# Attention and a hard-swish feed-forward in one kernel: buffers handed out by the plan, other tile addresses, halved first loads and last stores

## Chip, cores and metric

The kernel runs on one core of a Trainium2 chip. The metric is the device time of one execution in microseconds, the median of several runs of the same built program. A profiled execution gives a trace of every engine and of the transfers.

## What is computed

Causal attention over 4 batches of 12 heads (448 positions, 64 wide), then a feed-forward layer on the 1,792 tokens: `h = x @ w_in`, `g = h * relu6(h + 3) / 6`, `out = g @ w_out`.

```python
def _attn_ref(q, k, v):                       # (4, 12, 448, 64) each
    scores = scale * np.matmul(q, k.transpose(0, 1, 3, 2))
    mask = np.triu(np.ones((seq, seq), dtype=bool), k=1)
    scores = np.where(mask, -1000000000.0, scores)
    scores = scores - np.max(scores, axis=-1, keepdims=True)
    attn = np.exp(scores)
    attn = attn / (np.sum(attn, axis=-1, keepdims=True) + 1e-09)
    return np.matmul(attn, v)

def _moe_ref(x, w_in, w_out):                 # (1792, 768), (768, 2048), (2048, 768)
    h = x @ w_in
    relu6 = np.clip(h + 3.0, 0.0, 6.0)
    g = h * relu6 / 6.0
    return g @ w_out
```

## The kernel before

**The work.** Attention goes in 24 units, each one batch and one pair of heads (`unit(b, p)`). A unit loads q, k and v, computes scores for four row tiles of 112 positions (tiles 3, 2, 1, 0 with 448, 336, 224, 112 columns; L464), takes row minima on VectorE (L479), exponentials with row sums on ScalarE (L486), inverses (L496, L497), scales the rows (L505, L507), transposes the probabilities on TensorE into PSUM banks (L527), copies them into d tiles (L346 on ScalarE, L349 on VectorE) and multiplies them with v (L540). The first six units multiply q and k in full float32 with operands in `gh`; the others split q and k into a rounded and a rest part, each in d tiles.

The feed-forward works on transposed activations. A product is a triple of matmuls of 448 columns in the rounded type: high weights by high input (L614), high by low (L615), low by high (L616). The weights lie in `wh` and `wl` (a few in `pr2`). The input halves lie in d tiles (`x`, `xc`, `gt`, `gm`), but in `gh` and `gl` for the products of `early_products`. Batch 0 goes through both layers while attention is still running, batch 1's second layer is mixed with later work in `middle`, batches 2 and 3 go through `last_first` and `last_second`, which combine block products with seven products in place of eight. The weights come as 64-bit words, are put together by VectorE in PSUM banks (`words`, L577, L579, L582) and kept in HBM (`kept_w`, sums in `kept_s`, activations in `kept_g`, `kept_x`) for later use.

**The order.** Nothing is issued as it is written. Each operation is handed to a planner, `Flow`, with a key (a due time), the engines that may run it and their costs. `Flow.run` lets a clock run, takes for each free engine the ready operation with the lowest key and writes out one order for all engines; tables of numbers at the head (`UNIT`, `LOADS`, `WORDS`, `T_*`, `K_*`) set the keys. All loads and stores go through SyncE's one queue, only three of the last stores through ScalarE's.

**Buffers.** A `Buf` is a tile with a tag; the tag names a pool: 22 buffers `d`, 8 PSUM banks `b`, 6 `wd`, 3 `wh`, and so on (`BUFS`, `BANKS`). The planner holds an operation back until enough buffers of its tags are free, and counts them only. When the order is written out, `ap` asks the pool for a tile of the tag, and the pool gives one of its buffers. The pools lie one after another in memory in the order const, gh, gl, prow, r, kl, vr, wh, wl, pr2, pr1, wd, d; `SHIFT` puts an unused pad ahead of some.

Of the kernel before, what the change touches and what calls it, by code (L numbers as in the profile page):

```python
# [30 lines left out]
T_FIRST = -87  # L31
T_PACE = 4.5
# [4 lines left out]
T_LOAD = -12  # L37
T_W = 10
T_WLOAD = 4
T_XA = 146  # L40
T_X = 172
T_LAST = 180
# [6 lines left out]
M_LOAD = 18  # L49
E_WORDS = 6.5  # L50
K_SCORES = 0
K_TURN = 7
K_TURNS = 0.4
K_PRODUCT = 10
K_GATE = 6
KEEP_FULL = 4
# [3 lines left out]
A_FIRST = 6  # L60
D_FIRST = 0
T_V = 11
# [3 lines left out]
UNIT = [-75, -37, -5, 7, 4, 3.5, -3.5, -3.5, 1.5, 0, -1.5, -1.5, -2, -5, -0.5, -5.5, -3, -1.5, -7, -7.5, 0.5, -2, 0, -2.5]  # L66
LOADS = [8, -8, 8, 6, 4, -10, 6, 12, -14, -14, -2, 0, -24, -10, 4, 2, 0, -18, 12, 6, -10, 10, -20, 12]
# [3 lines left out]
WORDS = [-1, 6, -1, 5, -8, 5, 7, -1, -1, -6, 8, -7, -6, -5, 6, 8, -7, -3, -5, 8, 7, -3, -7, -5, 2, 8, -2, -5]  # L71
T_ISSUE = 0.36
NORM_LAG = 2
# [6 lines left out]
SHIFT = dict(wh=112, d=112)  # L80
# [5 lines left out]
MOST = dict(qk=3, op=4, wf=6, sf=6, x=8, pt=9, pr3=5, pr20=3, xq=6, xc=21, gt=12, gm=8, so=3, s=8, most=7, ps=8, mo=4, c=8)  # L86
# [4 lines left out]
class Buf:  # L91
    def __init__(self, kind, shape, dt):
        self.kind, self.uses = kind, KINDS.get(kind, kind).split()
        self.tag = self.uses[0]
        self.shape, self.dt, self.tile, self.refs, self.held = shape, dt, None, 0, False
# [10 lines left out]
class Flow:  # L106
# [10 lines left out]
    DMA_PACKET, DMA_RATE, DMA_LANES, DMA_LATENCY = 0.010, 21e3, 16, 2.1  # L117

    def __init__(self, slots):
        self.free = dict(slots)  # L120
        self.filler, self.idle, self.spare = None, 0.0, 1
        self.ops, self.wrote, self.readers = [], {}, {}
# [29 lines left out]
    def run(self):  # L152
# [82 lines left out]
    def fill(self, now, out):  # L235

        n = int((now - self.idle - self.SPARE_TIME) / self.FILL)
        if self.spare and self.FILL_FROM < self.idle and now < self.FILL_UNTIL:
            b = Buf("b", [128, 512], F32)
            for i in range(n):  # L240
                out.append((self.idle + self.FILL * i, len(out), "PE", lambda _, m=self.mode: self.filler(b, m), set()))
# [45 lines left out]
def tile_causal_attention_hardswish_moe(ctx: ExitStack, tc: tile.TileContext, q, k, v, w_in, w_out, out):  # L287
# [116 lines left out]
    def unit(b, p):  # L404
# [11 lines left out]
        for a, src in enumerate((q, k)):  # L416
            dma(
                t + T_LOAD + LOADS[at], 4 * S, lambda a=a: qa(a),
                lambda src=src: src[b, p].rearrange("e d s -> (e d) s"), w=[kq[a]],
            )  # L420
# [46 lines left out]
        for a, two in enumerate(((3, 2), (1, 0))):  # L467
# [4 lines left out]
                reads + [("unit", at - (2 if b else DEPTH))], True,  # L472
# [195 lines left out]
    def store(key, m, g, v, o, queues=("SP",)):  # L668
        rows, n = out[128 * m:128 * m + 128].rearrange("m (g h w) -> m g h w", g=B, h=len(queues)), S // len(queues)
        for h, queue in enumerate(queues):  # L670
            dma(key, 4 * n, lambda h=h: rows[:, g, h], lambda h=h: v()[:, n * h:n * h + n], [o], (), queue)

    def sixth(key, o, ok, acc, s_, sk):
# [305 lines left out]
    def last_second(g):  # L979
# [128 lines left out]
```

## Time and profile before

| | |
|---|---|
| median of 3 runs | 591.88 us (591.71 to 592.56) |
| the profiled execution | 593.77 us, its span 592.0 us |
| mean granted clock of TensorE | 0.996 of full |
| busy share of the span: TensorE, VectorE, ScalarE, GpSimd | 98%, 83%, 68%, 39% |
| moved by transfers | 115.59 MB, mean 195 GB/s |

The span goes from the first to the last instruction of the program; the profiled execution has some time outside it. A matmul's row in the trace begins when it starts, and its end is modelled, so successive rows overlap: the pace of a stream is read from starts. In the views, PE is TensorE's matmuls, PEld its weight loads, DVE VectorE, ACT ScalarE, POOL GpSimd, SP SyncE (SPq its queue of transfers).

### The profile page before, as it was taken

Reading aid. Unit: us, or ns where it says so; the run is one execution under the profiler, and the core shown is the slowest. Engines: PE = TensorE matmul, PEld = TensorE weight load, DVE = VectorE, ACT = ScalarE, POOL = GpSimd, SP = SyncE. Lnnn points to the kernel's source line nnn. Section 1 sums busy time; section 2 is a strip of 40 time slices with the busy share of each in tenths; the row PEclk is TensorE's granted clock in tenths of the full one; section 3 lists DMA queues with packets and bytes.
Section 4 is the critical chain, followed back from the end, with each engine's and each line's share of the span. In section 5 each row is a group of like instructions: output and inputs, shape, how many; then the busy total and the mean of one; then the engine's idle time right before and its main releaser. Section 6 shows DMA issues by size and latency. Waiting matters only on the chain.

```text
span 592.0 us, 10667 instructions
## 1 busy us (share of the span) xinstructions
PE 579.1 (98%) x3484; PEld 501.1 (85%) x3484; DVE 492.6 (83%) x1099; ACT 403.2 (68%) x966; POOL 232.8 (39%) x223
## 2 busy tenths in 40 slices
PE   6999999999999999999999999999999999999997
PEld 3667988988888798878988888999999999999996
DVE  6999988799598899859998688998988799975641
ACT  6987888776668767679978796465555486454530
POOL 2757987764635554667453121043100042100000
PEclk9999999999999999989999999999999999999999
DMA  8936999996779899985834434422211424443411
GB/s 271 348 153 241 347 335 402 313 297 212 243 260 329 257 373 311 336 268 161 295 100 138 144 105 132 145 89 82 79 54 53 124 66 132 144 119 110 137 58 47
DMA packets 61064, 115.59 MB, mean 195 GB/s; under 512 B 6480, under 2 KB 36304, under 8 KB 61008
## 3 DMA queue, kind: packets, MB, share of 16 engines
q1 hardware_dynamic: 60576, 114.57, 58.0%
q8 instruction: 27, 0.44, 0.3%
q10 hardware_dynamic: 432, 0.34, 0.2%
q14 instruction: 29, 0.24, 0.1%
HBM read 83.39 MB, written 31.49 MB: 194 GB/s over the span
## 4 chain that ended last, share of the span: by engine, by line
PE 83%; DVE 7%; DMA 5%; ACT 4%; issue 1%; SPq 0%; DVEq 0%; ACTq 0%
PE b L614 22%; PE b L616 21%; PE b L615 21%; PE b L540 7%; PE b L527 6%; PE b L464 5%; DVE b L479 3%; DMA wd<-in_w_out_dram 3%; ACT d L486 1%; DMA gl<-kept_g 1%; DMA kept_w<-d 1%; DVE prow L479 1%; ACT gl L486 1%; DVE b L577 1%; DVE b L579 1%
## 5 line engine op out<-in xcount | busy, mean ns | idle before, releaser
L614 PE MATMUL b<-d,wh 128*128 128x448 f32 x624 | 233.3, 374 | 0.1
L616 PE MATMUL b<-d,wl 128*128 128x448 f32 x624 | 226.7, 363 | 0.0
L615 PE MATMUL b<-d,wh 128*128 128x448 f32 x624 | 225.9, 362 | 0.0
L346 ACT CAST wh<-wd 128x768 fp32r<-128x768 f32 x88 | 73.9, 839 | 77.9 <-PE b L615 74.2
L616 PEld LDWEIGHTS b<-d,wl 128*128 128x128 f32 x624 | 116.8, 187 | 10.8
L614 PEld LDWEIGHTS b<-d,wh 128*128 128x128 f32 x624 | 117.1, 188 | 10.4 <-DVE d L349 0.5
L615 PEld LDWEIGHTS b<-d,wh 128*128 128x128 f32 x624 | 117.2, 188 | 8.0
L358 DVE TENSOR_TENSOR wl<-wd,wh 128x768 fp32r<-128x768 f32 x73 | 76.5, 1049 | 25.3 <-ACT wh L346 24.0
L479 DVE CUSTOM_DVE_ANT_0 b<-b,mask 112x448 f32<-112x448 f32 (+1 forms) x192 | 80.1, 481 | 18.8 <-PE b L464 17.3
L486 ACT ACTIVATE d<-b,prow 112x448 f32<-112x448 f32 (+1 forms) x144 | 72.2, 515 | 12.9 <-DVE prow L479 12.8
L527 PE MATMUL b<-ident,d 112*112 112x112 f32 x384 | 54.5, 261 | 2.1 <-ACT d L486 1.4
L358 POOL TENSOR_TENSOR wl<-d,wh 128x768 fp32r<-128x768 f32 (+1 forms) x28 | 45.5, 1629 | 24.4 <-ACT wh L346 22.6
L527 PEld LDWEIGHTS b<-ident,d 112*112 112x112 f32 x384 | 41.9, 133 | 6.8 <-ACT d L486 1.9
L358 POOL TENSOR_TENSOR d<-d 128x896 fp32r<-128x896 f32 (+2 forms) x22 | 36.0, 1638 | 26.1 <-DVE wl L358 11.3
L346 ACT COPY d<-b 112x336 f32<-112x336 f32 (+1 forms) x92 | 38.8, 492 | 8.3 <-PE b L527 4.9
L507 POOL TENSOR_SCALAR d<-d,prow 112x112 f32<-112x112 f32 (+2 forms) x59 | 29.4, 509 | 30.7 <-ACT d L486 11.4
L464 PE MATMUL b<-d 64*112 64x448 f32 (+3 forms) x432 | 37.4, 311 | 1.6 <-ACT d L346 1.6
L505 ACT ACTIVATE d<-d,prow 112x112 f32<-112x112 f32 (+2 forms) x76 | 37.9, 551 | 1.4 <-DVE prow L497 1.2
L540 PE MATMUL b<-d,vr 112*64 112x224 f32 (+3 forms) x288 | 38.4, 410 | 0.0
L464 PEld LDWEIGHTS b<-d 64*112 64x112 f32 x432 | 30.7, 174 | 8.6 <-issue 2.4
L540 PEld LDWEIGHTS b<-d,vr 112*64 112x64 f32 x288 | 19.3, 138 | 19.9 <-issue 12.4
L358 DVE TENSOR_TENSOR d<-d 128x512 f32<-128x512 f32 (+3 forms) x44 | 32.7, 753 | 2.8 <-ACT d L346 1.5
(108 smaller groups left out, 942.6 us busy)
## 6 DMA issues: line engine op xcount, KB each, us to landing
wd<-in_w_in_dram SPq DMA_DIRECT2D x32, 384.0 KB, 6.2
wd<-in_w_out_dram SPq DMA_DIRECT2D x24, 512.0 KB, 6.4
wd<-kept_w SPq DMA_DIRECT2D x32, 384.0 KB, 3.9
wd<-kept_s SPq DMA_DIRECT2D x32, 384.0 KB, 3.1
kept_w<-d SPq DMA_DIRECT2D x16, 384.0 KB, 6.1
kept_w<-d SPq DMA_DIRECT2D x24, 256.0 KB, 4.8
kept_s<-d SPq DMA_DIRECT2D x24, 256.0 KB, 5.2
wd<-kept_w SPq DMA_DIRECT2D x48, 128.0 KB, 2.3
```

What stands on the lines that cost most here:

```text
L346: nc.scalar.copy(o(), i()) if scale is None else nc.scalar.mul(o(), i(), scale)
L358: (nc.gpsimd if e == "P" else nc.vector).tensor_tensor(o(), a(), b(), op)
L464: nc.tensor.matmul(score(e, i), qx[m, c], kx[m, :w], start=n == 0, stop=n == len(terms) - 1)
L479: lambda _, e=e, i=i, w=w: nc.vector.tensor_tensor_reduce(score(e, i), score(e, i), mask[:, S - w:], -0.125, 3.0e38, ALU.add, ALU.min, ap( ...
L486: lambda _, e=e, i=i: nc.scalar.activation(row_of(pr, e, i), score(e, i), ACTF.Exp, bias=ap(st)[:, e, i:i + 1], scale=-1.0, accum_out=ap(s ...
L505: nc.scalar.mul(x, x, ap(st)[:, e, 4 + i:5 + i])
L507: (nc.gpsimd if w == "P" else nc.vector).tensor_scalar(x, x, ap(st)[:, e, 4 + i:5 + i], 1.0, ALU.mult, ALU.mult)
L527: nc.tensor.transpose(ap(tp)[:C, C * n:C * n + C], row_of(pr, e, i)[:, C * j:C * j + C], ident)
L540: nc.tensor.matmul(ap(av)[64 * e:64 * e + 64, S - w:S], va()[:, j, e, :], ap(ph)[:, e, o:o + w], start=(j == 0), stop=(j == NC_ - 1),)
L614: nc.tensor.matmul(ps, ap(wh)[:, a], xh, start=start, stop=False, skip_group_check=more)
L615: nc.tensor.matmul(ps, ap(wh)[:, a], xl, start=False, stop=False, skip_group_check=more)
L616: nc.tensor.matmul(ps, ap(wl)[:, a], xh, start=False, stop=stop, skip_group_check=more)
```

## The change

Five things change together.

1. **Buffers.** Every buffer has a pool tag of its own (`d0`, `d1`, ...) with one buffer. The planner keeps a queue of free buffers for each tag, gives the one that came free first, and `ap` asks for that one.
2. **Transfers.** The planner's clock holds SyncE's queue until the eighth transfer before has landed (`QUEUE`), and its prices for a transfer are lower.
3. **Addresses.** `SHIFT` changes: a pad of 64 words (256 bytes) ahead of `gh`, 112 words ahead of `wh` as before, 16 words (64 bytes) in place of 112 (448 bytes) ahead of `d`.
4. **First loads and last stores.** The first unit's q and k are loaded in two halves each, columns 0 to 224 and 224 to 448, and its narrow row tiles (1, 0) come first. The last sums of `last_second` are computed and stored in halves of 224 columns, the first half through ScalarE's queue and the second through SyncE's.
5. **Tables.** Nearly all numbers that set keys, and the limits on how many buffers a kind may hold (`MOST`), are others.

```diff
-T_FIRST = -87
-T_PACE = 4.5
+T_FIRST = -120
+T_PACE = 4
...
-UNIT = [-75, -37, -5, 7, 4, 3.5, -3.5, -3.5, 1.5, 0, -1.5, -1.5, -2, -5, -0.5, -5.5, -3, -1.5, -7, -7.5, 0.5, -2, 0, -2.5]
+UNIT = [-88, -19, 3, 4, 2, 0, -1.5, -3, 4.5, 4, -2.5, -3, -3.5, -8, -2.5, -4.5, -2, -1.5, -6, -4.5, -2.5, 1, -4.5, 2]
...
-SHIFT = dict(wh=112, d=112)
+SHIFT = dict(gh=64, wh=112, d=16)
...
-MOST = dict(qk=3, op=4, wf=6, sf=6, x=8, pt=9, pr3=5, pr20=3, xq=6, xc=21, gt=12, gm=8, so=3, s=8, most=7, ps=8, mo=4, c=8)
+MOST = dict(qk=3, op=4, wf=4, sf=6, x=8, pt=7, pr3=5, pr20=4, xq=6, xc=21, gt=12, gm=9, so=3, s=8, most=8, ps=8, mo=4, c=8)
...
-    DMA_PACKET, DMA_RATE, DMA_LANES, DMA_LATENCY = 0.010, 21e3, 16, 2.1
+    QUEUE = 8
+    DMA_PACKET, DMA_RATE, DMA_LANES, DMA_LATENCY = 0.008, 23e3, 16, 2.1
 
     def __init__(self, slots):
         self.free = dict(slots)
+        self.slots = {t: deque(range(n)) for t, n in slots.items() if t in BUFS or t in BANKS}
...
                 elif what == "end":
                     left -= 1
-                    for b in x.bufs:
+                    for b in sorted(x.bufs, key=lambda b: b.at):
                         b.refs -= 1
                         if not b.refs:
+                            self.slots[b.tag].append(b.slot)
                             for t in b.uses:
                                 self.free[t] += 1
...
-        for b in o.bufs:
-            b.held = True
+        for b in sorted((b for b in o.bufs if not b.held), key=lambda b: b.at):
+            b.held, b.slot = True, self.slots[b.tag].popleft()
...
+        if e == "SP":
+            self.landed.append(o.ends[-1])
+            t = max([t, *self.landed[-self.QUEUE:-self.QUEUE + 1]])
         busy[e] = t
...
-            b.tile = pools[b.tag].tile(b.shape, b.dt, tag=b.tag, name=b.tag)
+            b.tile = pools[b.tag].tile(b.shape, b.dt, tag=f"{b.tag}{b.slot}", name=b.tag, bufs=1)
...
+        cuts = [(0, 2 * C), (2 * C, S)] if at == 0 else [(0, S)]
+        halves_ = [[(*x, h) for x in kq] for h in range(len(cuts))]
+        for h, (lo, hi) in enumerate(cuts):
+            for a, src in enumerate((q, k)):
+                dma(
+                    t + T_LOAD + LOADS[at], 4 * (hi - lo), lambda a=a, lo=lo, hi=hi: qa(a)[:, lo:hi],
+                    lambda src=src, lo=lo, hi=hi: src[b, p].rearrange("e d s -> (e d) s")[:, lo:hi], w=[halves_[h][a]],
+                )
...
-        for a, two in enumerate(((3, 2), (1, 0))):
+        for a, two in enumerate(((1, 0), (3, 2)) if at == 0 else ((3, 2), (1, 0))):
...
         def finish(key, m, h, o, ok, acc, s_, sk, queues=("SP",)):
-            sixth(key, o, ok, acc, s_, sk)
-            store(key + .5, m, 2 + h, o, ok, queues)
+            n = S // len(queues)
+            for a, queue in enumerate(queues):
+                c = slice(n * a, n * a + n)
+                sixth(key, lambda c=c: o()[:, c], (*ok, a), acc, lambda c=c: s_()[:, c], sk, c)
+                dma(
+                    key + .5, 4 * n, lambda c=c: out[128 * m:128 * m + 128, S * (2 + h):S * (3 + h)][:, c],
+                    lambda c=c: o()[:, c], [(*ok, a)], (), queue,
+                )
```

The order at the program's start, on SyncE's queue, where q, k and v of the first units are loaded into `gh` and `gl`. Before:

```order
L337 DMA gh<-in_q_dram 128x448
L337 DMA gh<-in_k_dram 128x448
L337 DMA gl<-in_v_dram 112x512
L337 DMA gh<-in_q_dram 128x448
L337 DMA gh<-in_k_dram 128x448
```

And now:

```order
L349 DMA gh<-in_q_dram 128x224
L349 DMA gh<-in_k_dram 128x224
L349 DMA gh<-in_q_dram 128x224
L349 DMA gh<-in_k_dram 128x224
L349 DMA gl<-in_v_dram 112x512
L349 DMA gh<-in_q_dram 128x448
```

The first two loads are two times two, and the first v and the second unit's q come two places later.

On TensorE around the first projection triples: scores (from `gh`), triples (from d and wh, wl), then transposes (with `ident`). Before:

```order
L464 MATMUL b<-gh 112x112 x2
L614 MATMUL b<-d,wh 128x448
L615 MATMUL b<-d,wh 128x448
L616 MATMUL b<-d,wl 128x448
L614 MATMUL b<-d,wh 128x448
L615 MATMUL b<-d,wh 128x448
L616 MATMUL b<-d,wl 128x448
L614 MATMUL b<-d,wh 128x448
L615 MATMUL b<-d,wh 128x448
L616 MATMUL b<-d,wl 128x448
L464 MATMUL b<-gh 112x448 x2
```

And now, in the new line numbers (L480 for scores, L543 for transposes, L630 to L632 for triples):

```order
L480 MATMUL b<-gh 112x336 x2
L630 MATMUL b<-d,wh 128x448
L631 MATMUL b<-d,wh 128x448
L632 MATMUL b<-d,wl 128x448
L543 MATMUL b<-ident,d 112x112
L543 MATMUL b<-ident,gl 112x112
L543 MATMUL b<-ident,d 112x112 x2
L543 MATMUL b<-ident,gl 112x112
L543 MATMUL b<-ident,d 112x112 x2
L630 MATMUL b<-d,wh 128x448
L631 MATMUL b<-d,wh 128x448
L632 MATMUL b<-d,wl 128x448
```

Three triples stood together; now they stand one by one between the transposes of a unit. So it goes on until attention ends: a change from a triple to a transpose stands 30 times in the order before and 53 times now. The numbers of triples (696), transposes (480), scores and products with v are the same.

At the program's end on VectorE, the sums of the last products with the parts that wait in d. Before, the last row of sums, and now:

```order
-L358 TENSOR_TENSOR wl<-wd,wh 128x768 x2
-L675 SCALAR_TENSOR_TENSOR d<-b,d 128x448 x3
+L370 TENSOR_TENSOR wl<-wd,wh 128x768 x2
+L689 SCALAR_TENSOR_TENSOR d<-b,d 128x224 x6
```

Three sums of 448 columns have become six of 224.

## Rows read from the trace of the kernel before

**Rows 1.** Busy time by stretches: us, busy and instructions by engine, clock, DMA.

```profile
core 0: us, PE busy (x) PEld busy (x) DVE busy (x) ACT busy (x) POOL busy (x), PEclk, DMA share, GB/s
0.00:40.00 40.00, 33.12 (x228) 21.62 (x228) 31.98 (x126) 32.04 (x109) 21.38 (x43) 1.00 0.85 285
40.00:180.00 140.00, 140.00 (x920) 120.24 (x921) 123.39 (x299) 105.54 (x266) 95.31 (x81) 1.00 0.82 287
180.00:260.00 80.00, 78.00 (x529) 64.58 (x528) 68.40 (x182) 58.78 (x162) 47.00 (x43) 0.98 0.93 316
...
366.00:588.00 222.00, 222.00 (x1100) 205.71 (x1098) 177.25 (x276) 115.15 (x194) 27.76 (x22) 1.00 0.32 100
...
240.00:260.00 20.00, 18.41 (x112) 14.86 (x111) 14.99 (x40) 12.60 (x34) 14.42 (x12) 0.91 0.95 328
```

**Rows 2.** TensorE in order of time, first and last start, 14 triples apart.

```profile
143.40 0.36 PE L614 MATMUL b<-gh,wh 128*128 128x448 f32 x1
...
151.80 0.36 PE L614 MATMUL b<-gh,wh 128*128 128x448 f32 x1
```

**Rows 3.** Line L614: count, ns least/median/most, first and last start.

```profile
L614 PE MATMUL b<-d,wh x624: 360/367/478, 33.4 to 587.5; 128*128 128x448 f32 x156
L614 PE MATMUL b<-gh,wh x48: 361/363/477, 128.2 to 168.6; 128*128 128x448 f32 x48
```

**Rows 4.** The chain that ended last, its start (at us, us, what); one issue.

```profile
1.23 2.69 DMA gh<-in_k_dram
...
4.05 1.86 PE b L464 x4
...
6.01 0.63 DVE b L479
...
10.15 0.68 ACT d L486 x4
...
2.16 0.43 SPq L337 DMA_DIRECT2D gh<-in_q_dram  x1
```

**Rows 5.** In order of time around 252 us, and the landing of the store.

```profile
252.22 0.78 ACT L346 COPY d<-b 112x336 f32<-112x336 f32 x2 [3.22 <-DMA gl<-kept_g]
...
252.71 2.17 PE L464 MATMUL b<-d 64*112 64x448 f32 x11 [1.59 <-ACT d L346]
...
245.86 0.37 SPq L337 DMA_DIRECT2D kept_s<-d  x1
...
DMA to landing us min/median/max: 6.2/6.2/6.2
```

**Rows 6.** TensorE in order of time around 194 us.

```profile
193.35 0.71 PE L527 MATMUL b<-ident,d 112*112 112x112 f32 x2
194.28 0.31 PE L527 MATMUL b<-ident,pr 112*112 112x112 f32 x1 [0.21 <-DVE d L582]
```

**Rows 7.** The last sum, and the last stores: count, KB, us to landing.

```profile
588.30 0.62 DVE L675 SCALAR_TENSOR_TENSOR d<-b,d 128x448 f32<-128x448 f32 x1 [1.81 <-PE b L616]
...
out_dram<-d SPq DMA_DIRECT2D x3, 112.0 KB, 1.8
out_dram<-d ACTq DMA_DIRECT2D x3, 112.0 KB, 2.0
```

**Rows 8.** VectorE's first narrow minimum in order of time.

```profile
8.08 0.43 DVE L479 CUSTOM_DVE_ANT_0 b<-b,mask 112x224 f32<-112x224 f32 x1
```

**Rows 9.** TensorE in order of time: ten transposes, two triples, transposes again.

```profile
88.09 0.26 PE L527 MATMUL b<-ident,d 112*112 112x112 f32 x1
...
88.57 0.64 PE L527 MATMUL b<-ident,d 112*112 112x112 f32 x5
...
90.29 0.26 PE L527 MATMUL b<-ident,d 112*112 112x112 f32 x1
```

**Rows 10.** TensorE's wait for loads; landing of the q load issued at 241.4.

```profile
PE b L464 <- DMA gh<-in_k_dram: 4.1, 1, 4.1
...
DMA to landing us min/median/max: 8.8/8.8/8.8
```

More of the change, by code (lines that the diff above doesn't have):

```diff
@@ L1 @@
 from bisect import insort
+from collections import deque
 from contextlib import ExitStack
@@ L36 @@
 T_DENSE = 7.25
-T_LOAD = -12
+T_LOAD = -18
 T_W = 10
-T_WLOAD = 4
-T_XA = 146
+T_WLOAD = 8
+T_XA = 163
 T_X = 172
-T_LAST = 180
+T_LAST = 182
 T_PAIR = 10.5
@@ L48 @@
 T_WORDS = 77
-M_LOAD = 18
+M_LOAD = 11
 E_WORDS = 6.5
 K_SCORES = 0
[L52 to L56, printed above, removed]
+K_TURN = 6.5
+K_TURNS = 0.6
+K_PRODUCT = 14
+K_GATE = 4
+KEEP_FULL = 0
 KEEP_TILED = 7
@@ L59 @@
 DEPTH = 3
-A_FIRST = 6
+A_FIRST = 4.8
 D_FIRST = 0
-T_V = 11
+T_V = 15
 FINE = 3
@@ L65 @@
 W_BEHIND = 4
-UNIT = [-75, -37, -5, 7, 4, 3.5, -3.5, -3.5, 1.5, 0, -1.5, -1.5, -2, -5, -0.5, -5.5, -3, -1.5, -7, -7.5, 0.5, -2, 0, -2.5]
-LOADS = [8, -8, 8, 6, 4, -10, 6, 12, -14, -14, -2, 0, -24, -10, 4, 2, 0, -18, 12, 6, -10, 10, -20, 12]
+UNIT = [-88, -19, 3, 4, 2, 0, -1.5, -3, 4.5, 4, -2.5, -3, -3.5, -8, -2.5, -4.5, -2, -1.5, -6, -4.5, -2.5, 1, -4.5, 2]
+LOADS = [-6, -64, -24, 12, -14, -2, 6, -12, -6, -10, -4, -16, -10, 12, 2, 6, -12, 8, -2, -8, 2, 2, 0, 12]
 K_KEEP = -4
@@ L70 @@
 GATE_FROM = 1
-WORDS = [-1, 6, -1, 5, -8, 5, 7, -1, -1, -6, 8, -7, -6, -5, 6, 8, -7, -3, -5, 8, 7, -3, -7, -5, 2, 8, -2, -5]
+WORDS = [2, 3, 0, 8, -8, 5, -6, 4, 3, 3, 1, 3, 8, 5, -2, -8, 8, 6, 2, -7, -7, 3, 7, 7, 4, 0, -1, 1]
 T_ISSUE = 0.36
-NORM_LAG = 2
+NORM_LAG = 1.5
 A_LAG = 0
@@ L85 @@
 )
-MOST = dict(qk=3, op=4, wf=6, sf=6, x=8, pt=9, pr3=5, pr20=3, xq=6, xc=21, gt=12, gm=8, so=3, s=8, most=7, ps=8, mo=4, c=8)
+MOST = dict(qk=3, op=4, wf=4, sf=6, x=8, pt=7, pr3=5, pr20=4, xq=6, xc=21, gt=12, gm=9, so=3, s=8, most=8, ps=8, mo=4, c=8)
 ORDERED = dict(sf=3, wd=0, wh=1, wl=2, xq=3, xc=3, gt=3, gm=3, pr3=4, pr2=5, pr1=6, pr20=9, pt=7, op=8)
 class Buf:
+    made = 0
     def __init__(self, kind, shape, dt):
@@ L94, in __init__ @@
         self.tag = self.uses[0]
-        self.shape, self.dt, self.tile, self.refs, self.held = shape, dt, None, 0, False
+        self.shape, self.dt, self.tile, self.slot, self.refs, self.held = shape, dt, None, None, 0, False
+        Buf.made += 1
+        self.at = Buf.made
 class Op:
@@ L116 @@
     KEEP = KEEP_FULL, KEEP_TILED
-    DMA_PACKET, DMA_RATE, DMA_LANES, DMA_LATENCY = 0.010, 21e3, 16, 2.1
+    QUEUE = 8
+    DMA_PACKET, DMA_RATE, DMA_LANES, DMA_LATENCY = 0.008, 23e3, 16, 2.1
     def __init__(self, slots):
         self.free = dict(slots)
+        self.slots = {t: deque(range(n)) for t, n in slots.items() if t in BUFS or t in BANKS}
         self.filler, self.idle, self.spare = None, 0.0, 1
-        self.ops, self.wrote, self.readers = [], {}, {}
+        self.ops, self.wrote, self.readers, self.landed = [], {}, {}, []
     def op(self, key, ways, parts, r=(), tiled=False, nbytes=0):
@@ L237, in fill @@
         n = int((now - self.idle - self.SPARE_TIME) / self.FILL)
-        if self.spare and self.FILL_FROM < self.idle and now < self.FILL_UNTIL:
+        if self.spare and self.slots["b"] and self.FILL_FROM < self.idle and now < self.FILL_UNTIL:
             b = Buf("b", [128, 512], F32)
+            b.slot = self.slots["b"][0]
             for i in range(n):
@@ L301, in tile_causal_attention_hardswish_moe @@
             ctx.enter_context(tc.tile_pool(name=f"shift_{tag}", bufs=1)).tile([128, SHIFT[tag]], F32, name=f"shift_{tag}")
-        pools[tag] = ctx.enter_context(tc.tile_pool(name=tag, bufs=bufs))
+        pools[tag] = ctx.enter_context(tc.tile_pool(name=tag, bufs=1))
     for tag, bufs in BANKS.items():
-        pools[tag] = ctx.enter_context(tc.tile_pool(name=tag, bufs=bufs, space=bass.MemoryType.PSUM))
+        pools[tag] = ctx.enter_context(tc.tile_pool(name=tag, bufs=1, space=bass.MemoryType.PSUM))
     flow = Flow({**BUFS, **BANKS, **MOST})
@@ L415, in unit @@
             qa, kq = lambda a: ap(first_qk)[:, 2 * p + a], [(first_qk, 2 * p + a) for a in range(2)]
[L416 to L420, printed above, removed]
+        cuts = [(0, 2 * C), (2 * C, S)] if at == 0 else [(0, S)]
[6 more added lines that the diff above has]
+                )
+        kq = [x for y in halves_ for x in y]
         dma(t + T_LOAD + LOADS[at] + T_V, 512 * NC_, va, lambda: v[b, p], w=[kv], rows=C)
@@ L471, in unit @@
                 [(cost * C * (i + 1) + more, lambda i=i: products(i), [(ps[e, i][0], i) for e in range(2)] + [("turn",)]) for i in two],
-                reads + [("unit", at - (2 if b else DEPTH))], True,
+                (halves_[0] if at == a == 0 else reads) + [("unit", at - (2 if b else DEPTH))], True,
             )
@@ L666, in first_layer, with store, sixth @@
         return out if g else (gh, gl)
[L668 to L673, printed above, removed]
+    def store(key, m, g, v, o):
+        dma(key, 4 * S, lambda: out[128 * m:128 * m + 128, S * g:S * g + S], v, [o])
+    def sixth(key, o, ok, acc, s_, sk, c=slice(0, S)):
         def emit(_):
-            nc.vector.scalar_tensor_tensor(o(), ap(acc)[:, :S], 1.0 / 6.0, s_(), ALU.mult, ALU.add)
-        one(key, {"D": 1}, elem(S), emit, [(acc, 0), sk], [ok])
+            nc.vector.scalar_tensor_tensor(o(), ap(acc)[:, c], 1.0 / 6.0, s_(), ALU.mult, ALU.add)
+        one(key, {"D": 1}, elem(c.stop - c.start), emit, [(acc, 0), sk], [ok])
     def snap_m(key, o, ok, acc):
```

## The prediction

> **What bounds the kernel now.** I read the busy time by stretches first [rows 1]. TensorE works in all of 366 to 588 us (222.00 of 222.00) and in all of 40 to 180 (140.00 of 140.00); it misses 6.9 us before 40 and 2.0 between 180 and 260, and the last sum starts only at 588.30 [rows 7]. No other engine is full over a whole stretch: VectorE has 177 of the last 222 us. So after 40 us TensorE's own pace sets the end, and a change can gain in three places: the pace of a matmul, the start, the waits in the middle.
>
> The pace is read from starts, since the durations in the rows overlap. The projections go in triples of matmuls of 448 columns (L614 to L616), and after 366 there is nothing else: 1098 weight loads are 366 triples in 222.00 us, 0.6066 each [rows 1]. From 143.40 to 151.80 there are 14 triples: 8.40 / 14 = 0.6000 us [rows 2]. Shapes, types and granted clock (1.00) are the same; the first read their moving operand from tile d, the second from gh and gl. 624 triples read d (a few more have their weights in pr), 48 read gh and gl [rows 3].
>
> The start is a chain: k's load is issued at 1.23 us and takes 2.69, the four first records of the scores 1.86, then VectorE's row minima from 6.01, and ScalarE's exponentials of the unit until 10.83 [rows 4].
>
> In the middle the largest wait stands at 252.71: TensorE idles 1.59 us for a bank, ScalarE having idled 3.22 us before it could copy transposes into a d tile at 252.22 [rows 5]. The row names a load of kept_g; but a store kept_s<-d, issued at 245.86, took 6.2 us [rows 5] and so landed at about 252.06, when the copy could start. I read it so: the copy had been given the d buffer that this store was still reading. Behind the wait the clock fell to its lower level (1.2 GHz): the mean grant of the 20 us around is 0.91 [rows 1], so 0.09 x 20 = 1.8 us of full-speed time were withheld, part of it while TensorE idled. A second wait is a transpose at 194.28 that waits for VectorE's words to leave a bank: it starts 0.93 us after the pair before it began at 193.35 [rows 6], while two transposes want 0.19 (five in 0.48 from 88.09, [rows 9]).
>
> **The change, part by part.** *Same work.* The two orders hold the same matmuls, loads and stores but for the cuts named below, and move some copies between VectorE, ScalarE and GpSimd.
>
> *Other addresses.* The padding ahead of d shrinks from 448 to 64 bytes. As built, d begins at byte 147,648 of a partition before and 147,520 now, wh at 96,000 and 96,256, gh at 19,264 and 19,520. The distance from wh to d was 51,648 = 201 x 256 + 192 and is 51,264 = 200 x 256 + 64; from wh to gh it is -300 x 256 + 64 in both, to gl -188 x 256 + 64. Tiles and half tiles (3,584 and 1,792 bytes) are whole multiples of 256, so every d operand had remainder 192 and now has 64, which gh and gl had all along. If the pace hangs on the remainder, 624 triples gain 6.6 ns each: **-4.1 us**. Bounds: 0 (the pace belongs to the other layout of gh and gl) and -4.3 (the few with weights in pr too). I take -4.1, since gh and d triples stand in one stage with one kind of weights, and the remainder is what I find to differ besides the name.
>
> The Trainium skill ("TensorE: Matmul & The Clock Gate", Part 2, step 1) says that TensorE has two independent read ports, so that loading the next weights takes nothing from the running matmul; "SBUF — State Buffer", Who interferes with whom, says that TensorE waits on nobody. By that, the place of d against wh would not matter and this term would be 0. The trace has two paces in one execution [rows 1, 2], which these pages do not explain.
>
> *Halved first loads.* The first k load is still the second issue (1.23 us), but 112 KB instead of 224. Nearest rows: a 112 KB store lands in 1.8 us, this 224 KB load in 2.7 [rows 4, 7]; I take 2.25, so scores begin 0.45 earlier (0 to 0.9). The first product has 224 columns where it had 448, half of 1.86 us: 0.9 earlier again. So VectorE starts at about 4.7, not 6.01. It then does its four short minima (0.43 and less each, [rows 8]) until about 6.0 and waits for the wide product: the second half of k is the fourth issue (2.16, [rows 4]) and lands at 4.4, before the short products end at about 5.0; 5.0 + 1.86 = 6.9. The four wide minima (6.01 to 8.08 now, [rows 4, 8], 2.1 us) end near 9.0; before, the short ones then followed until 9.2. But ScalarE, which was 1.6 us behind VectorE at 10.83 with the short exponentials, has done these and has one or two wide ones left, some 1.0 us by estimate, so the unit's exponentials end at about 10.0: **-0.8 us**, bounds 0 and -1.8 (all of VectorE's earlier start). This goes to the end one for one if nothing in the first 40 us absorbs it, since TensorE is full after.
>
> *The order of the first 40 us.* Triples now stand between single banks of transposes, where they fill gaps. Idle there besides the first 4.05 is 2.8 us [rows 1]; I take **-0.5**, bounds 0 and -2.8. The price of the splitting: ten transposes and two triples take 2.20 us (88.09 to 90.29), while 10 x 0.096 (five in 0.48) and 2 x 0.607 are 2.17 [rows 9]; 0.03 us for a block, 23 blocks more in the whole order (53 changes from a triple to a transpose, 30 before): **+0.7**, bounds 0.3 and 0.9.
>
> *Buffers chosen by the plan.* Until now the plan only counted free buffers, and which one a tile got was the pool's affair. Now the plan hands out the one that has been free longest by its own clock, and that clock holds a transfer back until the eighth before it has landed. The wait at 252 is of the kind that this removes: 1.59 idle and half of the 1.8 of withheld clock, **-2.5 us**. Bounds: 0, and -5 if the wait at 194 (0.7), the rest of the 2.0 idle and the rest of the clock go too. What is late next is then VectorE, 0.86 busy in that stage [rows 1].
>
> *Halved last stores.* The last sum of 448 columns took 0.62 us, then two stores of 112 KB land in 1.8 (SP) and 2.0 (ACT) [rows 7]. Now ACT's store leaves after half the sum, some 0.23 earlier (the difference of 448 and 224 columns: 0.63 - 0.43 is 0.20, [rows 4, 8]), and SP's leaves some 0.15 later but is the shorter: **-0.1**, bounds -0.2 and +0.2.
>
> Sum: -4.1 - 0.8 - 0.5 + 0.7 - 2.5 - 0.1 = -7.3 us. The profiled execution took 593.77 (span 592.0, the rest outside), 1.9 above the median 591.88 of the runs; differences carry over, so 591.9 - 7.3 = **584.6 us**.
>
> **Rivals.** *The remainder means nothing.* The fast triples differ also in that their two halves lie in two tiles. Then -4.1 falls away: 588.7. For it: the rows differ in both respects. Against it: a second tile is only another address, which is what the remainder is too. 0.15. The pages named above stand on this rival's side.
>
> *Time given back before 366.* TensorE comes earlier to a stage in which transfers (0.93 of their time between 180 and 260) and VectorE set the pace; the early gains become waits. What stays is behind 366, where TensorE is full with 366 triples: 366 x 6.6 ns = 2.4 and the tail 0.1: 589.4. For it: ScalarE and VectorE waits in [rows 5, 6]; against it: TensorE is full from 40 to 180 and the waits between 180 and 260 are 2.0 in all [rows 1]. 0.13.
>
> *A late load: slower.* In the new order all q and k loads stand at other places of SP's one queue. With the queue full, a q load takes 8.8 us to land [rows 10]; SP's later transfers wait behind it, ScalarE or GpSimd waits to split it, and the scores behind them. If one pair comes a full queue late in the stage 180 to 260 with no triples left to fill, the price is up to 8.8; with the other terms (-4.8 without the wait at 252) 595.9. It decides from a wait of 4.8 us on. Against it: TensorE waited for a load only once, 4.1 us at the start [rows 10]. 0.09.
>
> *The pools do nothing.* The d buffer was free anyway, other waits arise as large: -2.5 and -0.5 fall away, 587.6. 0.05.
>
> **How the numbers follow.** The forecast has 0.58 and stands for 580 to 588. A run of this kernel tells 0.2% (1.2 us) from no change. Faster: the forecast 0.58, the pools' rival 0.05, nine tenths of the remainder's (0.13), two thirds of the time given back (0.09): 0.85. Same 0.07, from the rest of these two and the light end of the late load; slower 0.08. Range: 579.5 (head and middle at their better bounds in part) to 590.0, which takes in the rivals at 588.7 and 589.4 and leaves out the late load and the tails, under 0.2.
>
> **What would show it.** Starts of 33 triples behind 366: 19.80 us apart (right) or 20.02. First score near 3.6 and first minimum near 4.7 us; the first unit's exponentials done near 10.0. Between 180 and 366 no idle above 0.5 us on TensorE and a granted clock of 1.00. A wrong prediction would show as new idle time on TensorE before scores (L480) with a load as releaser, or as triples at 0.607.

## The result and the profile after

The changed kernel took 586.63 us (median of 4 runs, 585.31 to 588.1), the kernel before 592.22 beside it (591.71 to 592.56): a ratio of 0.9907, 95% interval 0.9881 to 0.9933, or 5.6 us less. 584.6 had been forecast, with 579.5 to 590.0 as the range. The profiled execution took 586.24, its span 584.1; that of before 593.77 and 592.0. So the two profiled executions differ by 7.5 us, near the 7.3 of the forecast's sum, and the medians by 5.6: the profiled execution of before lay 1.55 above its median, that of the changed kernel 0.4 below.

Busy time by stretches of the changed kernel, to be laid beside [rows 1]:

```profile
core 0: us, PE busy (x) PEld busy (x) DVE busy (x) ACT busy (x) POOL busy (x), PEclk, DMA share, GB/s
0.00:40.00 40.00, 31.49 (x213) 20.40 (x214) 31.41 (x125) 29.57 (x102) 22.38 (x43) 1.00 0.91 274
40.00:180.00 140.00, 139.65 (x936) 119.61 (x936) 120.69 (x309) 108.63 (x282) 101.29 (x89) 1.00 0.78 272
180.00:260.00 80.00, 79.82 (x548) 67.79 (x546) 69.90 (x170) 60.95 (x165) 47.52 (x42) 1.00 0.96 324
240.00:260.00 20.00, 20.00 (x139) 16.43 (x140) 19.69 (x43) 17.67 (x46) 14.84 (x13) 1.00 1.03 355
```

Three things are to be seen. The stage from 180 to 260 has lost its idle time (79.82 busy, 78.00 before) and its fall of the clock (1.00 in 240 to 260, 0.91 before). The first 40 us have become worse, not better: TensorE works 31.49 us of them, and it worked 33.12. And what the busy time can't tell, the pace, stands in the starts. TensorE in order of time, two triples 33 apart:

```profile
399.99 0.36 PE L630 MATMUL b<-d,wh 128*128 128x448 f32 x1
...
419.79 0.36 PE L630 MATMUL b<-d,wh 128*128 128x448 f32 x1
```

33 triples in 19.80 us are 0.6000 each, the pace that only gh and gl had before [rows 2].

The start, from the timelines of TensorE, VectorE and ScalarE (start, duration, what, idle time ahead and its releaser):

```profile
3.48 3.69 PE L480 MATMUL b<-gh 64*112 64x224 f32 x16 [3.48 <-DMA gh<-in_k_dram]
8.69 2.15 PE L480 MATMUL b<-gh 64*112 64x448 f32 x16 [1.53 <-DMA gh<-in_k_dram]
...
23.77 1.57 PE L480 MATMUL b<-gh 64*112 64x448 f32 x6 [1.33 <-DVE d L598]
...
5.06 0.40 DVE L495 CUSTOM_DVE_ANT_0 b<-b,mask 112x224 f32<-112x224 f32 x1 [3.41 <-PE b L480]
...
9.57 0.56 ACT L502 ACTIVATE d<-b,prow 112x336 f32<-112x336 f32 x1
```

The first score starts at 3.48 (4.05 before), the first minimum at 5.06 (6.01) and the unit's last exponential ends at 10.13 (10.83, [rows 4]). So far the halves did nearly what was forecast. But then TensorE waits 1.53 us for the second unit's k, which it had not waited for, and 1.33 us at 23.77 for VectorE to leave a bank. VectorE was late there itself: it had waited for a load before each half of the first weight's words, and the words keep the bank. The same words before, and now:

```profile
19.17 1.05 DVE L577 TENSOR_SCALAR b<-wd 128x384 int32<-128x384 int32 x2
```

```profile
20.72 0.56 DVE L593 TENSOR_SCALAR b<-wd 128x384 int32<-128x384 int32 x1 [1.19 <-DMA wd<-in_w_in_dram]
21.77 0.56 DVE L593 TENSOR_SCALAR b<-wd 128x384 int32<-128x384 int32 x1 [0.49 <-DMA wd<-in_w_in_dram]
...
23.17 1.01 DVE L598 SCALAR_TENSOR_TENSOR d<-wd,b 128x384 int32<-128x384 int32 x2
```

The chain that ended last shows the same of the next weight. Behind the first scores it was VectorE's and ScalarE's work before [rows 4], and now its start is transfers, each issued when another one ahead of it had landed:

```profile
5.96 6.57 DMA gh<-in_q_dram
...
12.55 7.13 DMA gl<-in_v_dram
...
19.69 9.29 DMA wd<-in_w_in_dram
...
29.00 0.56 DVE b L593
```

VectorE begins the second half of the second weight's words only at 29.00, when this load has landed.

### The profile page after: what moved, and what is told of

It reads as the page before. It is cut to its first block, busy times and chain, and to the rows that moved or that the text cites. A ratio compares the mean times of both kernels' runs of the same rounds, so it can differ in the third digit from the quotient of the medians.

```text
span 584.1 us, 10651 instructions
## 1 busy us (share of the span) xinstructions
PE 571.7 (98%) x3484; PEld 500.3 (86%) x3484; DVE 485.5 (83%) x1091; ACT 402.9 (69%) x970; POOL 240.0 (41%) x230
## 3 DMA queue, kind: packets, MB, share of 16 engines
HBM read 83.39 MB, written 31.49 MB: 197 GB/s over the span
## 4 chain that ended last, share of the span: by engine, by line
PE 91%; DMA 4%; DVE 2%; ACT 2%; SPq 1%; issue 0%; DVEq 0%
PE b L630 24%; PE b L631 24%; PE b L632 24%; PE b L556 7%; PE b L543 6%; PE b L480 6%; DMA wd<-in_w_in_dram 2%; DMA gl<-in_v_dram 1%; DMA gh<-in_q_dram 1%; ACT d L502 1%; SPq L349 1%; DVE b L595 0%; DVE b L593 0%; ACT gl L502 0%; DVE d L598 0%
## 5 line engine op out<-in xcount | busy, mean ns | idle before, releaser
L630 PE MATMUL b<-d,wh 128*128 128x448 f32 x624 | 231.4, 371 | 0.2 <-ACT d L502 0.2
L632 PE MATMUL b<-d,wl 128*128 128x448 f32 x624 | 225.5, 361 | 0.0
L630 PEld LDWEIGHTS b<-d,wh 128*128 128x128 f32 x624 | 117.2, 188 | 10.5 <-issue 0.7
L632 PEld LDWEIGHTS b<-d,wl 128*128 128x128 f32 x624 | 116.8, 187 | 8.3
L370 DVE TENSOR_TENSOR wl<-wd,wh 128x768 fp32r<-128x768 f32 x70 | 72.7, 1039 | 28.7 <-ACT wh L358 27.8
L495 DVE CUSTOM_DVE_ANT_0 b<-b,mask 112x224 f32<-112x224 f32 (+1 forms) x192 | 80.2, 480 | 12.4 <-PE b L480 10.7
L502 ACT ACTIVATE d<-b,prow 112x448 f32<-112x448 f32 (+2 forms) x144 | 72.3, 516 | 15.6 <-DVE prow L495 13.8
L543 PE MATMUL b<-ident,d 112*112 112x112 f32 x384 | 56.1, 260 | 1.1 <-ACT d L502 0.8
L358 ACT COPY d<-b 112x336 f32<-112x336 f32 (+1 forms) x103 | 44.4, 487 | 12.8 <-PE b L543 8.3
L370 POOL TENSOR_TENSOR d<-d 128x896 fp32r<-128x896 f32 (+3 forms) x24 | 39.7, 1658 | 22.3 <-PE b L543 10.5
L370 POOL TENSOR_TENSOR wl<-wd,wh 128x768 fp32r<-128x768 f32 x18 | 33.1, 1841 | 35.3 <-ACT wh L358 33.5
L543 PEld LDWEIGHTS b<-ident,d 112*112 112x112 f32 x384 | 42.8, 133 | 5.0 <-POOL gl L523 1.0
L523 POOL TENSOR_SCALAR d<-d,prow 112x336 f32<-112x336 f32 (+2 forms) x62 | 33.0, 543 | 15.3 <-DVE prow L513 13.1
L370 POOL TENSOR_TENSOR d<-gh,d 128x448 fp32r<-128x448 f32 x8 | 9.6, 1201 | 71.3 <-DVE gh L370 55.6
L593 DVE TENSOR_SCALAR b<-wd 128x384 int32<-128x384 int32 (+1 forms) x56 | 33.2, 615 | 4.9 <-DMA wd<-in_w_in_dram 3.0
L521 ACT ACTIVATE d<-d,prow 112x112 f32<-112x112 f32 (+2 forms) x69 | 34.0, 528 | 4.5 <-DVE prow L513 4.2
L480 PEld LDWEIGHTS b<-d 64*112 64x112 f32 x432 | 30.2, 172 | 6.0 <-issue 2.0
```

The source lines that it names most:

```text
L358: nc.scalar.copy(o(), i()) if scale is None else nc.scalar.mul(o(), i(), scale)
L370: (nc.gpsimd if e == "P" else nc.vector).tensor_tensor(o(), a(), b(), op)
L480: nc.tensor.matmul(score(e, i), qx[m, c], kx[m, :w], start=n == 0, stop=n == len(terms) - 1)
L495: lambda _, e=e, i=i, w=w: nc.vector.tensor_tensor_reduce(score(e, i), score(e, i), mask[:, S - w:], -0.125, 3.0e38, ALU.add, ALU.min, ap( ...
L502: lambda _, e=e, i=i: nc.scalar.activation(row_of(pr, e, i), score(e, i), ACTF.Exp, bias=ap(st)[:, e, i:i + 1], scale=-1.0, accum_out=ap(s ...
L521: nc.scalar.mul(x, x, ap(st)[:, e, 4 + i:5 + i])
```

## The experiments

Each run has the kernel before beside it on the same chip; ratios are to that. Differences in us are of medians; the ratios and their intervals are worked out from all the runs, and since the kernel before has more runs in which the clock fell than some of the others, they can show about 1 us more. The address and pool kernels were chosen so that the order of instructions stays what it is, engine by engine, and only the cause in dispute differs.

**The place of d.** Four kernels. One number in the kernel before:

```diff
-SHIFT = dict(wh=112, d=112)
+SHIFT = dict(wh=112, d=16)
```

> The kernel before with one number changed: the pad ahead of d is 16 words, not 112, so that d begins 64 bytes (and not 192) past a multiple of 256 counted from wh; the order of every engine is that of before. Theory A (the remainder sets the pace): 33 triples behind 366 us are 19.80 us apart, not 20.02, and the time is 592.2 - 4.1 = 588.1. Theory B (gh and gl were faster for another reason, the place of d means nothing): 20.02 and 592.2.

Measured: 589.32 us, ratio 0.9942 (0.9918 to 0.9967), 2.9 less; three of the six runs, with a mean granted clock of 0.999 or more, took 588.1 to 588.5. And the number put back in the changed kernel:

```diff
-SHIFT = dict(gh=64, wh=112, d=16)
+SHIFT = dict(gh=64, wh=112, d=48)
```

> The changed kernel with d's pad at 48 words, so that d has its old remainder of 192 from wh; the order and the pools are those of the changed kernel. Theory A: triples of d at 0.6066 us again and 586.6 + 4.1 = 590.7. Theory B: 0.600 and 586.6. If the new pace comes from the pools or from the order, B's numbers too.

Measured: 589.34, ratio 0.9953 (0.9925 to 0.9981), 2.7 more than the changed kernel had taken on its own chip. Starts of 33 triples, of the first kernel and of the second:

```profile
399.95 0.36 PE L614 MATMUL b<-d,wh 128*128 128x448 f32 x1
...
419.75 0.36 PE L614 MATMUL b<-d,wh 128*128 128x448 f32 x1
```

```profile
399.79 0.36 PE L630 MATMUL b<-d,wh 128*128 128x448 f32 x1
...
419.81 0.36 PE L630 MATMUL b<-d,wh 128*128 128x448 f32 x1
```

19.80 and 20.02 us: the pace follows the pad, in either order and with either kind of pools. The rival that the remainder means nothing is out. Whose remainder it is, the third kernel asks, with `wh=144` in the place of `wh=112`:

> The changed kernel with wh's pad at 144 words, not 112: wh, wl and d all move by 128 bytes, gh and gl stay. d's own address now has remainder 192 (that of before), but its distance from wh still 64; gh's own remainder stays 64, but its distance from wh becomes 192. Theory A1 (the distance between the moving operand and the weights counts): d triples stay at 0.600, the 48 of gh and gl go to 0.607, 586.6 + 0.3 = 586.9. Theory A2 (the moving operand's own address counts): d triples go to 0.607, gh's stay at 0.600, 590.7.

Measured: 585.6, ratio 0.9884 (0.9866 to 0.9902). Two triples 33 apart that read d, and two 12 apart that read gh and gl:

```profile
399.64 0.36 PE L630 MATMUL b<-d,wh 128*128 128x448 f32 x1
...
419.44 0.36 PE L630 MATMUL b<-d,wh 128*128 128x448 f32 x1
...
154.68 0.36 PE L630 MATMUL b<-gh,wh 128*128 128x448 f32 x1
...
161.96 0.36 PE L630 MATMUL b<-gh,wh 128*128 128x448 f32 x1
```

d stays at 19.80 / 33 = 0.6000, and gh, which nobody moved, goes to 7.28 / 12 = 0.6067. The distance between the moving operand and the weights counts, not the operand's own place. This kernel also gives the term its best timing, since the kernel with `d=48` ran on the same chip: 589.34 - 585.6 = 3.7 us, and 576 more slow triples (624 of d less 48 of gh and gl) at 6.6 ns are 3.8. The fourth kernel has `d=0`, a distance of whole multiples of 256:

> The changed kernel with no pad ahead of d: its own remainder is 0 and its distance from wh is 0 too. No row of before has this case. Theory A: if what counts is that moving operand and weights don't fall on the same place, the triples are at 0.607 or more and the time is 590.7 or more. Rival: any remainder but 192 is as good, 0.600 and 586.6.

Measured: 590.68, ratio 0.9976 (0.9947 to 1.0005).

```profile
399.55 0.36 PE L630 MATMUL b<-d,wh 128*128 128x448 f32 x1
...
419.61 0.36 PE L630 MATMUL b<-d,wh 128*128 128x448 f32 x1
```

20.06 / 33 = 0.6079, the slowest of the three remainders that were tried (64, 192, 0), and the time is that of theory A. The remainder 128 was not tried.

**The pools.** Part 1 alone in the kernel before (its core; the free queues are those of the change's diff):

```diff
-            b.tile = pools[b.tag].tile(b.shape, b.dt, tag=b.tag, name=b.tag)
+            b.tile = pools[b.tag].tile(b.shape, b.dt, tag=f"{b.tag}{b.slot}", name=b.tag, bufs=1)
```

> The kernel before with part 1 alone: every buffer a pool of its own, given out by the plan; the planner's prices, the tables and the order of every engine are those of before, instruction for instruction, and so are the addresses. Theory P (the middle waits come from the pool giving a buffer that is still being read): the wait of 1.59 us at 252 and the one at 194 go, no idle time over 0.5 us between 180 and 366; where the clock doesn't fall before either, 592.2 - 2.5 = 589.7. Rival (the plan's own clock is wrong and the waits belong to the order): the wait at 252 stands, 592.2.

Measured: 590.29, ratio 0.994 (0.9915 to 0.9966), 2.7 less. Busy time of the stretch in which the 1.59 us were lost, and ScalarE's copies there, which came 3.22 us late before [rows 5]:

```profile
240.00:260.00 20.00, 20.00 (x129) 17.22 (x130) 16.28 (x46) 14.70 (x44) 15.40 (x14) 1.00 1.01 362
...
250.52 0.78 ACT L354 COPY d<-b 112x336 f32<-112x336 f32 x2 [0.41 <-PE b L535]
```

TensorE is busy in all of it, at the full clock, and the copies wait for TensorE's transposes alone. So a buffer was what they had waited for. All buffers changed at once, but two transfers alone come into question, the load that the row in [rows 5] names and the store that the forecast took in its place. The load's issue and landing before, and the store's with the pools:

```profile
246.91 0.32 SPq L337 DMA_DIRECT2D gl<-kept_g  x1
...
DMA to landing us min/median/max: 5.7/5.7/5.7
```

```profile
245.66 0.37 SPq L345 DMA_DIRECT2D kept_s<-d  x1
...
DMA to landing us min/median/max: 6.6/6.6/6.6
```

The load landed at 252.6, after the copies had begun at 252.22, so they had not waited for it. The store still lands late with the pools, at 252.3, but the copies begin at 250.52 without it. That fits the buffer under the store; which buffer a tile got, no trace names. Both parts together, the pools and `d=16`, in the old order with the old loads and stores:

> The kernel before with part 1 and the new place of d (pad 16 words), the old order, loads and stores. If the two terms add: 592.2 - 3.5 (d's new place as measured alone, 592.2 to 588.4 where the clock was full) - 2.5 = 586.2, the whole gain without the new tables and the halved loads. If the changed kernel's gain needs its tables: 588.5.

Measured: 586.71, ratio 0.988 (0.9837 to 0.9924). The two terms add (0.9942 x 0.994 = 0.988), and they are as much as the whole change. Then the other way round, the changed kernel with the old pools (the line above taken back):

> The changed kernel with the old pools (22 buffers of d in one pool, 8 banks in one, and so on, given in turn); the order of every engine is that of the changed kernel, instruction for instruction. Theory P: buffers come late, waits on TensorE of 2.5 us or more in all return between 40 and 366, 586.6 + 2.5 = 589.1. Rival (the new tables and the queue of eight made the order good, the pools give nothing): 586.6.

Measured: 585.57, ratio 0.9857 (0.9811 to 0.9902), not slower than the changed kernel. TensorE's waits of this kernel between 180 and 366 us (total, times, longest):

```profile
PE b L630 <- ACT d L502: 0.7, 1, 0.7
PE b L543 <- DVE d L598: 0.2, 1, 0.2
PE b L480 <- DVE gh L665: 0.2, 1, 0.2
```

1.1 us in all and no fall of the clock. The changed kernel itself waits 0.2 there in its first profile, but in a second one (of its repetition, below) it is 1.35 short of the 186 us, with waits of 0.70 and 0.57:

```profile
180.00:366.00 186.00, 184.65 (x1255) 159.19 (x1254) 159.49 (x385) 149.69 (x394) 94.06 (x82) 1.00 0.74 245
...
188.99 0.28 PE L543 MATMUL b<-ident,d 112*112 112x112 f32 x1 [0.57 <-DVE d L598]
```

So the old pools wait no more than the new ones in this order. Theory P holds in the old order and falls in the new one: there the transfers and copies meet no buffer that is still being read for long, whoever gives it.

**The first loads.** The changed kernel, the first unit's q and k sent whole, VectorE's, ScalarE's and TensorE's order untouched:

```diff
-                    t + T_LOAD + LOADS[at], 4 * (hi - lo), lambda a=a, lo=lo, hi=hi: qa(a)[:, lo:hi],
-                    lambda src=src, lo=lo, hi=hi: src[b, p].rearrange("e d s -> (e d) s")[:, lo:hi], w=[halves_[h][a]],
+                    t + T_LOAD + LOADS[at], 4 * (hi - lo), lambda a=a: qa(a),
+                    lambda src=src: src[b, p].rearrange("e d s -> (e d) s"), w=[halves_[h][a]], skip=h == 1,
```

With `skip` the second half's transfer is left out.

> The changed kernel, but the first unit's q and k come as two transfers of 224 KB, not four of 112; the order of all engines but SyncE is unchanged, SyncE's later transfers go out two places earlier. Theory L (the two more places cost more than the earlier first score gives): the first score starts at 4.05 and not 3.48, the second unit's k lands 0.9 us earlier than 8.56, and TensorE gets to the first projection about 1 us earlier; 585.6 or the same as the changed kernel within the measurement. Rival (the halves bring what they were forecast to bring): 586.6 + 0.8 = 587.4.

Measured: 583.86 (583.8 to 585.25), ratio 0.9837 (0.9793 to 0.9881), the lowest of all. (It ran on the chip of the pools' kernels, without the changed kernel beside it; the intervals of the two ratios touch at 0.9881.) Its first 40 us, its waits for loads there, and the chain's weight load:

```profile
0.00:40.00 40.00, 34.78 (x237) 23.05 (x238) 33.51 (x134) 31.17 (x108) 24.99 (x47) 1.00 0.86 274
...
PE b L480 <- DMA gh<-in_k_dram: 4.1, 1, 4.1
...
13.12 7.00 DMA wd<-in_w_in_dram
20.21 0.57 DVE b L593
```

The first score starts 0.6 later (4.09), and TensorE then never waits for k again; the second half of the first weight's words, the chain's here, begins at 20.21 (21.77 with the halves), TensorE does not wait for them, and it works 34.78 us of the 40, 3.3 more than with the halves. How much of this is the halves and how much one execution's luck, the other kernels tell: with halved columns TensorE worked between 30.58 and 34.38 us of the first 40 in seven profiled executions (mean 32.6), with the old order 33.1 to 33.3 in four, with whole loads in the new order 34.78 and 34.70. In two of the seven the clock fell within the 40 us, and there the same work is busy for longer. Both profiles with whole loads are of the shortest execution of their kernel. Faster loads alone don't explain them, though: the kernel with `wh=144`, with halves, moved 272 GB/s in its first 20 us, the one with whole loads 265, and still worked 1.0 us less of the 40:

```profile
0.00:20.00 20.00, 14.61 (x98) 10.15 (x99) 14.27 (x62) 14.94 (x54) 8.37 (x22) 1.00 0.92 272
0.00:40.00 40.00, 33.76 (x236) 22.88 (x237) 33.36 (x132) 31.17 (x108) 24.84 (x47) 1.00 0.86 274
```

```profile
0.00:20.00 20.00, 14.98 (x91) 9.47 (x92) 14.27 (x62) 14.22 (x53) 8.38 (x22) 1.00 0.92 265
```

Three kernels ask why, with the changed kernel beside them on the same chip:

> The changed kernel itself, unaltered, so that it is timed on the same chip as the three beside it: 586.6 by its first runs, 585.3 to 588.1 from run to run. Its head (first 40 us) varies with the rate of the loads, so the first w_in should land anywhere from 19 to 21 us.

Measured: 586.5 (584.69 to 589.15), ratio 0.9899 (0.9871 to 0.9927). Its profiled execution had the wait at 23.6 us again (1.22), and behind it the clock fell, as it fell behind the wait at 252 before:

```profile
20.00:40.00 20.00, 18.72 (x128) 11.78 (x125) 17.91 (x64) 15.49 (x51) 14.49 (x22) 0.91 0.87 301
```

The first profile of the changed kernel had the same wait (1.33) and kept a clock of 1.00. Next, halves by heads:

```diff
-                    t + T_LOAD + LOADS[at], 4 * (hi - lo), lambda a=a, lo=lo, hi=hi: qa(a)[:, lo:hi],
+                    t + T_LOAD + LOADS[at], 4 * (hi - lo), lambda a=a, h=h: qa(a)[64 * h:64 * h + 64] if at == 0 else qa(a),
```

(and the source's rows in the same way).

> The changed kernel, but the first unit's q and k are halved by rows (64 partitions of 448 columns, one head each) and not by columns; four transfers as before, their packets twice as long; all orders are unchanged, the first score now waits for whole columns. Theory Q (the halves cost two places of the eight transfers in flight): as the changed kernel, 586. Theory S (the halves cost by their short packets of 896 bytes): as with whole loads, 584.

Measured: 587.67 (585.71 to 589.55), ratio 0.9908 (0.9883 to 0.9933). Packets twice as long brought nothing, neither in the time (586.5 for the changed kernel beside it) nor in the first 40 us (32.88 us of work, at a clock of 0.96). That speaks against theory S and for theory Q, but settles neither: the first score came later too (4.29), and theory S's 584 is the whole loads' time on another chip, which the next kernel did not reach here. Then, with whole loads, v of the first unit behind q and k of the second:

> The changed kernel with whole first loads (as the run before at 583.9), and the first unit's v goes out behind the second unit's q and k, not ahead of them. Theory K (TensorE's wait for the second unit's k is on the path): that k lands 0.9 us earlier, 583.9 - 0.9 = 583.0. Rival W (the path of the first 40 us goes through the weights, which land as before, so the wait only moves): 583.9.

Measured: 587.08 (584.79 to 587.55), ratio 0.9897 (0.9875 to 0.992). Neither number came. The profile of its first 40 us is that of the whole loads:

```profile
0.00:40.00 40.00, 34.70 (x237) 23.61 (x238) 33.42 (x134) 31.16 (x108) 24.96 (x47) 1.00 0.87 274
```

That profiled execution took 584.79, but the other five runs took 586.8 to 587.6. So it stays open whether whole loads are worth 2.6 us in most executions, as their first run says, or are so only when the loads come fast, or lose it when v goes later. Of those five no trace exists.

**The last stores.** The last sum in one piece, its two stores as they are:

```diff
-                sixth(key, lambda c=c: o()[:, c], (*ok, a), acc, lambda c=c: s_()[:, c], sk, c)
+                if a == 0:
+                    sixth(key, o, ok, acc, s_, sk)
```

> The changed kernel with the last sums of 448 columns in one piece, their two stores of 224 columns as they are. The forecast's term was -0.1 for the halves. From the last matmul to the end of the span it was 3.8 us in the kernel before and 3.4 in the changed one: if the halves did this, 3.8 returns here and the time is 0.4 longer, 587.0; if the time outside the span (1.7 before, 2.1 after) goes the other way, the time is the same.

Measured: 586.58 beside 586.5 for the changed kernel itself. VectorE's last sum and the stores behind it, of the changed kernel:

```profile
580.79 0.69 DVE L689 SCALAR_TENSOR_TENSOR d<-b,d 128x224 f32<-128x224 f32 x2 [1.71 <-PE b L632]
581.22 0.34 ACTq L349 DMA_DIRECT2D out_dram<-d  x1
581.51 0.33 SPq L349 DMA_DIRECT2D out_dram<-d  x1
```

ScalarE's store leaves 0.43 us after the sum's start, where a whole sum alone takes 0.62 [rows 7]. From the last sum's start the span goes on for 3.3 us here (580.79 to 584.1) and for 3.7 in the kernel with one sum (580.34 to 584.0); but the time outside the span is 2.1 here (586.24 - 584.1) and 1.7 there (585.69 - 584.0). The time outside was 1.68 to 1.75 in all six runs with one sum, and 2.05 to 2.15 in all ten of the changed kernel. What the halves take from the span comes back behind it.

## Why the prediction was right, and where it was wrong

**Addresses: right.** -4.1 was forecast from 6.6 ns a triple. The pace is 19.80 us for 33 triples, and the pad alone moves it in both kernels. Of the three timings two, -2.9 and +2.7, lie at the small end: the interval of the first goes from 2.0 to 4.9 us. The third, on one chip, gave 3.7 where 3.8 was due. Tile d's distance from the weights is the cause, shown by gh, which took the slow pace when only wh moved. The Trainium skill ("TensorE: Matmul & The Clock Gate", Part 2, step 1) holds that the read port of the weights is independent of that of the moving operand; "SBUF — State Buffer", Who interferes with whom, that TensorE waits on nobody. By both the distance would not matter. The trace differs: 0.6000, 0.6067 or 0.6079 us for the same triple, by the distance of the two, and the measurement decides. What in the memory or the ports does it, no run here shows.

**Halved first loads: the step that failed.** -0.8 was forecast, on the condition that nothing in the first 40 us absorbs the earlier start. The start was sized nearly rightly: the first score was to come near 3.6 (3.48), the exponentials were to end near 10.0 (10.13). Only the first minimum, due near 4.7, came at 5.06: from the first score to it 1.58 us passed, 1.96 before, so the shorter products saved 0.4 there and not 0.9. But two more transfers stand ahead of all others in the one queue, and I had costed only the loads that became shorter. SyncE issues one every 0.47 us; two timelines' rows, of the changed kernel and of that with whole loads, have the second unit's k:

```profile
3.59 0.43 SPq L349 DMA_DIRECT2D gh<-in_k_dram  x1
```

```profile
2.64 0.43 SPq L349 DMA_DIRECT2D gh<-in_k_dram  x1
```

0.95 us later, and it took 5.0 us to land in the one and 5.3 in the other. Later loads can only follow landings: the fifteenth issue of the changed kernel waits until 8.58, when this k, the seventh, has landed.

```profile
8.58 0.33 SPq L349 DMA_DIRECT2D gh<-in_k_dram  x1
```

The first 40 us lost 1.6 us of TensorE's work in the first profile (33.12 to 31.49) where they were to gain 1.3 less the splitting. In the whole loads' profile the same stretch gains 1.7 over before (34.78 - 33.12). The term was of the wrong sign in the profiles: all seven with halved columns lie below both with whole loads. Its size in the median is open, as said above. In the rivals I had the late load as one mechanism, at 180 to 260 us; it came at the start, where I had not looked for it, and at less than its price.

**The order of the first 40 us.** -0.5 was forecast, and with whole loads the profiles show -1.6 and -1.7: of the right sign, and too small. The splitting of triples and transposes (+0.7) is not to be told apart in any run; TensorE's stage from 40 to 180 is 0.35 us short of full in the changed kernel's first profile.

**Buffers chosen by the plan: right in size, in part by luck, and not what the change lives on.** -2.5 was forecast, 1.59 idle and 0.9 of clock, and the pools alone in the old order gave -2.7; the wait at 252 went, as read. But the median execution had no fall of the clock to give back: against those of before on that chip with a granted clock of 0.999 or more (median 592.56) the pools still gave 2.3, and what brought more than the idle time no trace tells. The rival "the pools do nothing" is wrong there. In the new order it is right: the old pools cost nothing (585.57), because the new tables no longer bring about that wait. So pools and tables each remove the wait at 252, and together they remove it once. Where both are in one change, neither has a term of its own. Between 180 and 260 TensorE idled 2.0 us before and 0.4 with the pools alone; in the changed kernel it was 0.2 in one profile and 1.35 in the other, so the new tables have lesser waits of their own there. The forecast's sign, no idle time above 0.5 from 180 to 366, held in the first of these profiles and not in the second (0.70 and 0.57). The wait at 194 did not go with the pools (a transpose at 195.40 us in the kernel with the pools alone starts 0.87 after the pair ahead of it, 0.93 in [rows 6]). In the changed kernel's first profile no such wait is left, but in the second TensorE waits 0.57 at 188.99 for the same step of VectorE's words, so the tables don't remove it each time.

**The last stores.** -0.1 was forecast within 0.2. The medians with and without the halves are 0.1 apart, which the runs, spread over 3 to 5 us, can't tell from nothing.

**The sum.** With the old order, pools and address alone make 586.71. So the new tables, halved loads and halved stores together add nothing that the runs can tell, where -0.7 was forecast for the head, the splitting and the end. The forecast's -7.3 held for the profiled executions, which had the clock's fall in the one and not in the other; that the two agree so well is luck. I had let differences carry over from a profiled execution to the median, though half of the withheld clock was a term of the sum. Of 44 further executions of the kernel before, 14 had a mean granted clock of 0.997 or less and took 593.4 to 597.9; the others took 591.1 to 593.6. The median execution had no such fall to give back. The sum is 1.7 us more than the medians' difference (7.3 and 5.6). The head with the splitting and the end, 0.7, came to nothing; the addresses gave 0.4 to 1.4 less than 4.1; and 0.9 of clock was not there, though the pools' term as a whole came out. How these share the 1.7 the runs don't tell.

## What to carry to other kernels

Where TensorE is full, read its pace from starts and group it by the distance in memory between moving operand and weights: a pad of some words, which costs nothing, was worth 1.1% of a triple here, and one run shows it. A load that is split to start earlier also takes a place in its queue; follow that queue to the first load of the next unit before counting the gain. A wait that depends on which buffer is handed out can go by another order as well as by other pools, so such terms are not added.

## What the runs showed of the hardware

The pace by distance: 0.6000 us a triple at 64 bytes past a multiple of 256, 0.6067 at 192, 0.6079 at 0.

The rate of the first loads differs from execution to execution with the same loads in the same order: the changed kernel moved 241 and 247 GB/s in the first 20 us of two executions, those that differ from it only in a pad of d or wh 226 to 272. TensorE was at work for 30.58 to 33.76 us of the first 40 in these five.

A wait of 1.2 to 1.6 us on TensorE cost more in some executions than in others, since the clock fell behind it (0.91 over 20 us) or did not (1.00), with the same wait in both. Where no such wait was left (the pools with the pad, 4 runs; the whole loads, 4 runs) no run had a mean granted clock below 0.999; of the ten with the pools alone, whose profile shows no such wait either, one had 0.997. With v going later, where the one profile shows none, three of six runs had 0.997; what happened in them no trace tells.
